# Attention feeding a gated MLP on one core: DMA transposes moved ahead of a store, score units moved by one place, batch 1 reordered, the last products in single banks

## Chip, cores, metric

One Trainium2 chip, one core. The metric is the device time of one execution in microseconds (us). Kernels that are compared ran on the same chip in alternating rounds. A ratio is the mean time of one kernel's runs over that of the other's runs of the same rounds, so it is not quite the ratio of the medians quoted beside it. The clock quoted with a run is the mean share of full speed that was granted to TensorE.

Engine names: PE is TensorE, PEld its weight loads, DVE VectorE, ACT ScalarE, POOL GpSimd, SP SyncE, which issues nearly all DMAs. SPq is the SP queue.

## The reference, cut

```python
# attention: q (8,16,384,64), k and v (8,4,384,64); 4 q heads share one kv head
attn = softmax(q @ k.T / sqrt(64));  a = attn @ v          # -> x (8, 384, 1024)
# gated MLP with a spatial mix over the sequence
h = relu(x @ w_in);  u, v = h[..., :512], h[..., 512:]
v_n = (v - mean(v)) / sqrt(var(v) + 1e-6)
v_s = einsum('ts,bsd->btd', w_spatial, v_n) + b_spatial
out = (u * v_s) @ w_out
```

## The kernel before

The eight batches overlap. While batch `b` computes its scores (18 "units": two matmuls on PE, then one exp on ACT), PE does the MLP of batches `c = b-1` and `d = b-2` between the units. Scores go through two PSUM buffers, so unit n needs the exp of unit n-2 to be over. Most products are made in two halves of 64 rows that run side by side; between the halves PE waits for a mark that POOL sets. q and k of batches 2 to 7 are cast by POOL and transposed by DMA, issued from SP.

```python
def batch(b, p, q, r, s):                 # p..s: PSUM banks
    group_uu(d, 2, 3, units(1, 3), (r, s))
    if more:
        cast_all_k(b + 1)
    unit(b, 3)
    value(c, 2, (p, q, r))
    # ... cut: units 4 to 12, value products, stores 1 and 2 of batch d,
    #          cast_all_q(b+1, 0), cast_all_q(b+1, 1), norm(c)
    if more:
        cast_v(b + 1, nc.gpsimd)
    group_voo(b, 0, d, 4, 5, units(13, 15), (p, s, r))   # its last copy issues store 3 of batch d
    if more:
        dma_transposes(b + 1)                            # k, q, q
    if b + 2 < B:
        load_all(b + 2)
    p, q, r, s = q, s, p, r
    group_sp(c, (units(15, 16), units(16, 17)), (p, q, r, s))

    def between():
        unit(b, 17)
        if more:
            unit(b + 1, 0)

    group_uu(c, 0, 1, between, (p, q))

# tail, last batch c: both spatial products of a pair share one two-bank tile
u_mm(c, 0)
sc = [ps_sc.tile([P, 2, 512], FP32, ...) for i in range(2)]
for m in range(NDT):
    sp_mm(c, m, sc[m // 2][:, m % 2, :])      # PE, 3 matmuls
    sp_add(c, m)                              # DVE
gate(c, 0)
for mu in range(1, NDT):
    u_mm(c, mu); gate(c, mu)
for i in range(6):
    o_mm(c, i)
    o_copy(c, i, nc.scalar if i % 2 else nc.vector, store_half=i >= 4)
```

The softmax here doesn't subtract the row's maximum and nothing guards it: scores larger than these inputs give would overflow.

## Time and profile before

| | before |
|---|---|
| median of four runs (range) | 278.56 us (277.77 to 279.52) |
| profiled span | 276.8 us |
| PE busy | 247.0 us, 89% |
| length of batches 2 to 6, from one batch's first value product to the next's | 30.05, 31.08, 31.41, 31.05, 32.34 us |

The lines that carry the argument stand in the prediction below. In a row of the table of waits the numbers are the sum in us, the times, and the longest. In a row of the timeline they are the start in us, the length in us, engine, line, operation, out<-in, and in brackets the idle time just before and what ended it. A row of the stretches gives from:to, the length, and the busy time of PE, PEld, DVE, ACT and POOL with counts, then the TensorE clock, the DMA share and GB/s.

### The profile page before, as it was taken

How to read it: one execution, taken by the hardware profiler on the slowest of the kernel's cores; microseconds unless marked ns; L12 is line 12 of the kernel's file. 1: busy time of each engine (PE TensorE's matmuls, PEld its weight loads, DVE VectorE, ACT ScalarE, POOL GpSimd, SP SyncE). 2: the span in 40 equal slices, each digit the busy share in tenths (PEclk: the TensorE clock that was granted, in tenths of full speed). 3: DMA queues.
4: the chain of work that ended last, by engine and by line, in shares of the span. 5: the costliest groups of instructions: out<-in, count | busy, mean ns of one | idle time of the engine just before them, and what ended most of it. 6: DMA issues, size and time to landing. Idle time of an engine off the chain costs nothing.

```text
span 276.8 us, 6011 instructions
## 1 busy us (share of the span) xinstructions
PE 247.0 (89%) x2529; PEld 116.2 (42%) x2529; DVE 150.0 (54%) x274; ACT 183.7 (66%) x228; POOL 47.9 (17%) x114
## 2 busy tenths in 40 slices
PE   2888698989997999899997999889995999989794
PEld 1232343544454444554454444554453444544351
DVE  2436569634584357625684357724683465836352
ACT  2978867879774787667774787668774777623402
POOL 3518114012300223012300123012300000000000
PEclk9999999999999999999999999999999999999999
DMA  8998999900129811693129811593229011100505
GB/s 220 279 315 209 238 254 234 321 14 11 69 117 255 267 78 76 169 291 104 78 116 233 290 78 75 164 297 103 79 108 188 0 78 75 79 2 0 229 0 227
DMA packets 57434, 41.66 MB, mean 151 GB/s; under 512 B 26816, under 2 KB 53568, under 8 KB 57408
## 3 DMA queue, kind: packets, MB, share of 16 engines
q1 hardware_dynamic: 53648, 37.89, 44.6%
q0 software_dynamic: 2720, 3.15, 6.9%
q8 instruction: 19, 0.31, 0.5%
q10 hardware_dynamic: 1040, 0.26, 0.4%
q14 instruction: 7, 0.06, 0.1%
HBM read 25.95 MB, written 12.58 MB: 139 GB/s over the span
## 4 chain that ended last, share of the span: by engine, by line
PE 78%; DMA 8%; DVE 6%; ACT 5%; issue 1%; SPq 0%; POOLq 0%; POOL 0%; ACTq 0%
PE sc L259 12%; PE po L491 11%; PE pv L451 11%; PE X L280 11%; PE pu L464 10%; DMA qT<-q 7%; PE sums L280 6%; PE psp L477 5%; ACT aT L270 4%; PE pv L319 4%; PE po L414 4%; PE pu L389 3%; DVE v_s L379 2%; DMA q<-in_q_dram 1%; DVE v_n L353 1%
## 5 line engine op out<-in xcount | busy, mean ns | idle before, releaser
L270 ACT ACTIVATE aT<-sc 128x1024 f16<-128x1024 f32 x144 | 141.2, 1023 | 53.6 <-PE sc L259 51.3
L259 PE MATMUL sc<-qT,kT 64*128 64x512 f16 x288 | 55.0, 392 | 14.9 <-DMA qT<-q 8.6
L491 PE MATMUL po<-w_out,gT 64*128 64x512 f16 x288 | 68.1, 376 | 0.0
L451 PE MATMUL pv<-w_in,xt 64*128 64x512 f16 x272 | 66.0, 376 | 0.0
L432 DVE COPY osb<-po 128x512 f32<-128x512 f32 x39 | 26.8, 688 | 30.3 <-PE po L491 26.7
L464 PE MATMUL pu<-xt,w_in 64*128 64x384 f16 x416 | 39.3, 323 | 2.0 <-DVE v_s L379 1.5
L401 DVE SCALAR_TENSOR_TENSOR gT<-pu,v_s 128x384 f16<-128x384 f32 x32 | 16.6, 553 | 41.3 <-PE pu L464 37.8
L307 DVE TENSOR_TENSOR xt<-X,rec 128x512 f16<-128x512 f32 x48 | 30.9, 686 | 12.5 <-ACT rec L299 11.0
L280 PE MATMUL X<-aT,v 128*32 128x512 f16 x576 | 36.5, 389 | 0.4 <-DVE osb L432 0.4
L259 PEld LDWEIGHTS <-kT 64*128 64x128 f16 x288 | 17.2, 94 | 43.7 <-issue 32.8
L528 POOL MEMSET mark<- 1x1 f32 x45 | 4.9, 108 | 165.4 <-PE po L491 87.6
L491 PEld LDWEIGHTS <-gT 64*128 64x128 f16 x288 | 25.5, 94 | 16.6 <-POOL mark L528 4.6
L451 PEld LDWEIGHTS <-xt 64*128 64x128 f16 x272 | 24.7, 94 | 14.1
L464 PEld LDWEIGHTS <-w_in 64*128 64x128 f16 x416 | 22.2, 94 | 17.2 <-issue 5.0
L168 POOL CAST q<-q 128x768 f16<-128x768 f32 (+2 forms) x32 | 23.6, 768 | 22.9 <-DMA q<-in_q_dram 21.4
L298 ACT ACTIVATE rec<-sums 128x512 f32<-128x512 f32 x24 | 14.5, 604 | 13.6 <-PE sums L280 13.6
L280 PEld LDWEIGHTS <-v 128*32 128x32 f16 x576 | 16.0, 99 | 16.9 <-issue 2.3
L280 PE MATMUL sums<-aT,ones 128*32 128x512 f16 x288 | 20.6, 392 | 0.1
L477 PE MATMUL psp<-wsT,v_n 64*128 64x384 f16 x168 | 18.7, 322 | 0.2 <-DVE wsT L206 0.2
L379 DVE TENSOR_TENSOR v_s<-psp,bias_b 128x384 f32<-128x384 f32 x28 | 16.9, 673 | 2.3 <-PE psp L477 2.3
L331 DVE TENSOR_SCALAR v_r<-pv 128x512 f32<-128x512 f32 x17 | 11.7, 691 | 9.5 <-PE pv L319 5.4
L340 DVE BATCH_NORM_STATS2 stats<-v_r 128x6 f32<-128x512 f32 x24 | 16.6, 690 | 0.2
(44 smaller groups left out, 165.7 us busy)
## 6 DMA issues: line engine op xcount, KB each, us to landing
out_dram<-osb SPq DMA_DIRECT2D x23, 512.0 KB, 2.7
q<-in_q_dram SPq DMA_DIRECT2D x14, 768.0 KB, 7.5
v<-in_v_dram SPq DMA_DIRECT2D x8, 384.0 KB, 8.6
k<-in_k_dram SPq DMA_DIRECT2D x7, 384.0 KB, 3.9
w_in<-in_moe_w_in_dram POOLq DMA_DIRECT2D x8, 256.0 KB, 7.6
q<-in_q_dram SPq DMA_DIRECT2D x2, 512.0 KB, 5.1
w_out<-in_moe_w_out_dram POOLq DMA_DIRECT2D x2, 512.0 KB, 14.4
ws<-in_moe_w_spatial_dram SPq DMA_DIRECT2D x1, 576.0 KB, 7.7
```

The costliest lines, as they stand in the source:

```text
L168: engine.tensor_copy(dst, src)
L259: mm = nc.tensor.matmul(sc[:, half, :], kT[b][lo:hi, gp, t, :], rhs[lo:hi, :], start=True, stop=True)
L270: nc.scalar.activation(aT[b, qt][:, gp, t], held["sc", b, u], AF.Exp, scale=scale)
L280: nc.tensor.matmul(dst[32 * g : 32 * (g + 1), :], weights(t, g), a[:, g // 2, t, g % 2, :], start=(t == 0), stop=(t == NST - 1),)
L307: nc.vector.tensor_tensor(xt[:, jj, :, qt * P : (qt + 1) * P], held["X", b, qt, jj].rearrange("p (j q) -> p j q", j=G), held["rec", b, qt] ...
L340: nc.vector.bn_stats(s6, held["v_r", b, st])
L379: nc.vector.tensor_tensor(held["v_s", b][:, m, :].rearrange("p (t s) -> p t s", t=NST), held["psp", b, m][:, 0:S].rearrange("p (t s) -> p ...
L432: nc.vector.tensor_copy(osb[:, cols], held["po", b, i])
L451: yield lambda kc=kc: nc.tensor.matmul(held["pv", b, st], xT[b][rows, kc, st * P : (st + 1) * P], w_in16[rows, kc, DH:DFF], start=(first a ...
L464: yield lambda kc=kc: nc.tensor.matmul(held["pu", b, mu][:, 0:S], w_in16[rows, kc, mu * P : (mu + 1) * P], xT[b][rows, kc, :], start=(firs ...
L477: yield lambda st=st: nc.tensor.matmul(held["psp", b, m][:, 0:S], held["v_n", b, st][rows, m * P : (m + 1) * P], wsT16[rows, st, :], start ...
L491: yield lambda m=m: nc.tensor.matmul(held["po", b, i], held["gT", b][rows, m, tt * P : (tt + 1) * P], w_out16[rows, m, half * 512 : (half ...
```

## The change

The intent: the transposes no longer stand behind a store that waits for compute; PE gets something to do in each short wait that is left. The core of the diff, cut:

```diff
 # part 1 and 2, batch()
-        group_uu(d, 2, 3, units(1, 3), (r, s))
+        group_uu(d, 2, 3, units(2, 4), (r, s))
         if more:
             cast_all_k(b + 1)
-        unit(b, 3)
         value(c, 2, (p, q, r))
 ...
             cast_v(b + 1, nc.gpsimd)
+            dma_transposes(b + 1)
         group_voo(b, 0, d, 4, 5, units(13, 15), (p, s, r))
-        if more:
-            dma_transposes(b + 1)
 ...
+        unit(b, 17)
+
         def between():
-            unit(b, 17)
             if more:
                 unit(b + 1, 0)
+                unit(b + 1, 1)
 # and the caller
-        banks = 0, 1, 2, 3
+        banks = 3, 0, 2, 1
 # part 3, batches 0 and 1: spatial weights cast by POOL, q/k transposes two to a bank,
 # a v product of batch 0 moved up, unit 16 ahead of a v product, unit (2, 1) added at the end
-            nc.vector.tensor_copy(
+            nc.gpsimd.tensor_copy(
                 ws16[:, tt, :, :], ws32[:, tt, :].rearrange("p (s t) -> p t s", t=NST)
 ...
-        for gp in range(NGP):
-            transpose_q(1, gp, 1)
+        transpose_q2(1, 1)
+        one[3]()
+        transpose_ws(0, 2)
         xmul(0, 2)
-        v_full(0, 1)
-        one[3]()
+        transpose_ws(2, 3)
 # part 4, tail
-        u_mm(c, 0)
-        sc = [ps_sc.tile([P, 2, 512], FP32, name=f"sc_sp_{i}", tag="sc") for i in range(2)]
+        sc = ps_sc.tile([P, 2, 512], FP32, name="sc_u", tag="sc")
+        u_mm(c, 0, sc[:, 0, :])
         for m in range(NDT):
-            sp_mm(c, m, sc[m // 2][:, m % 2, :])
+            sp_mm(c, m)
             sp_add(c, m)
-        gate(c, 0)
+            if m == 0:
+                gate(c, 0)
 ...
-        for i in range(2 * NST):
+        o_mm(c, 0, 0, 3)
+        o_mm(c, 1, 0, 3)
+        for i in range(2):
+            o_mm(c, i, 3, 4)
+            o_copy(c, i, nc.scalar if i % 2 else nc.vector)
+        for i in range(2, 5):
             o_mm(c, i)
-            o_copy(c, i, nc.scalar if i % 2 else nc.vector, store_half=i >= 4)
+            o_copy(c, i, nc.scalar if i % 2 else nc.vector, store_half=i == 4)
+        last_o(c, 5)      # two halves of 256 columns; the second stored from ACT's queue
```

More of the change, by code (lines that the diff above doesn't have):

```diff
@@ L199, in cast_ws, with transpose_ws @@
         loaded["ws16"] = ws16
-    def transpose_ws(st):
+    def transpose_ws(s0, s1):
         ws16 = loaded["ws16"]
-        psw = bank([P, NST, P], FP16, f"psw_{st}")
-        for tt in range(NST):
-            nc.tensor.transpose(psw[:, tt, :], ws16[:, tt, st, :], ident16)
-        nc.vector.tensor_copy(wsT16[:, st, :].rearrange("p (t q) -> p t q", t=NST), psw)
+        psw = bank([P, s1 - s0, NST, P], FP16, f"psw_{s0}")
+        for st in range(s0, s1):
+            for tt in range(NST):
+                nc.tensor.transpose(psw[:, st - s0, tt, :], ws16[:, tt, st, :], ident16)
+        nc.vector.tensor_copy(
+            wsT16[:, s0:s1, :], psw.rearrange("p s t q -> p s (t q)")
+        )
     def new_kT(b):
@@ L248, in transpose_q, with transpose_k2, transpose_q2 @@
         nc.vector.tensor_copy(qT[b, gp][:, qt], pq)
+    def transpose_k2(b):
+        k16 = loaded["k16", b]
+        pk = bank([P, NGP, NST, P], FP16, f"pk_{b}")
+        for gp in range(NGP):
+            for t in range(NST):
+                nc.tensor.transpose(
+                    pk[:, gp, t, :], k16[:, gp, t, :, :].rearrange("p h d -> p (h d)"), ident16
+                )
+        new_kT(b)
+        nc.vector.tensor_copy(kT[b], pk)
+    def transpose_q2(b, qt):
+        pq = bank([P, NGP, G, P], FP16, f"pq_{b}_{qt}")
+        for gp in range(NGP):
+            q16 = loaded["q16", b, gp]
+            for j in range(G):
+                nc.tensor.transpose(
+                    pq[:, gp, j, :], q16[:, qt, j, :, :].rearrange("p h d -> p (h d)"), ident16
+                )
+        for gp in range(NGP):
+            if (b, gp) not in qT:
+                new_qT(b, gp)
+            nc.vector.tensor_copy(qT[b, gp][:, qt], pq[:, gp])
     def score_mm(b, u):
@@ L384, in sp_add, with u_mm @@
         )
-    def u_mm(b, mu):
-        pu = bank([P, 512], FP32, f"pu_{b}_{mu}")
+    def u_mm(b, mu, dst=None):
+        pu = bank([P, 512], FP32, f"pu_{b}_{mu}") if dst is None else dst
         for kc in range(NKT):
@@ L408, in gate, with o_mm @@
         )
-    def o_mm(b, i):
+    def o_mm(b, i, m0=0, m1=NDT):
         tt, half = i // 2, i % 2
-        po = bank([P, 512], FP32, f"po_{b}_{tt}_{half}")
-        for m in range(NDT):
+        if m0 == 0:
+            held["po", b, i] = bank([P, 512], FP32, f"po_{b}_{tt}_{half}")
+        for m in range(m0, m1):
             nc.tensor.matmul(
-                po,
+                held["po", b, i],
                 held["gT", b][:, m, tt * P : (tt + 1) * P],
@@ L420, in o_mm @@
             )
-        held["po", b, i] = po
     def o_copy(b, i, engine=None, store_half=False):
@@ L437, in o_copy, with last_o @@
             nc.sync.dma_start(rows, osb)
+    def last_o(b, i):
+        tt, half = i // 2, i % 2
+        osb = held["osb", b, tt]
+        rows = out[b].rearrange("(p t) d -> p t d", t=NST)[:, tt, :]
+        for n in range(2):
+            cols = slice(half * 512 + n * 256, half * 512 + (n + 1) * 256)
+            po = bank([P, 256], FP32, f"po_{b}_{tt}_{half}_{n}")
+            for m in range(NDT):
+                nc.tensor.matmul(
+                    po,
+                    held["gT", b][:, m, tt * P : (tt + 1) * P],
+                    w_out16[:, m, cols],
+                    start=(m == 0),
+                    stop=(m == NDT - 1),
+                )
+            if n:
+                nc.scalar.activation(osb[:, cols], po, AF.Copy)
+                nc.scalar.dma_start(rows[:, cols], osb[:, cols])
+            else:
+                nc.vector.tensor_copy(osb[:, cols], po)
+                nc.sync.dma_start(rows[:, cols], osb[:, cols])
     LO, HI = slice(0, D), slice(D, P)
@@ L655, in first_batch @@
             if vi == 8:
-                for gp in range(NGP):
-                    transpose_k(1, gp)
-                    transpose_q(1, gp, 0)
+                transpose_k2(1)
+                transpose_q2(1, 0)
+                v_mm(0, 1)
+                relu(0, 1, nc.vector)
+                stats(0, 1)
+                cast_ws()
     def load_all(b):
@@ L690, in second_batch @@
         one[2]()
-        for gp in range(NGP):
-            transpose_q(1, gp, 1)
+        transpose_q2(1, 1)
+        one[3]()
+        transpose_ws(0, 2)
         xmul(0, 2)
-        v_full(0, 1)
-        one[3]()
+        transpose_ws(2, 3)
         load_all(2)
@@ L703, in second_batch @@
         one[5]()
-        for gp in range(NGP):
-            transpose_q(1, gp, 2)
-        cast_ws()
+        transpose_q2(1, 2)
         one[6]()
@@ L712, in second_batch @@
         norm(0)
-        for st in range(NST):
-            transpose_ws(st)
         one[8]()
@@ L719, in second_batch @@
         group_sp(0, one[11:13])
+        dma_transposes(2)
         value(1, 1)
@@ L722, in second_batch @@
         xmul(1, 1)
-        dma_transposes(2)
         load_all(3)
@@ L730, in second_batch @@
         group_uu(0, 0, 1, between)
+        one[16]()
         v_full(1, 1)
-        one[16]()
         one[17]()
         unit(2, 0)
+        unit(2, 1)
     def batch(b, p, q, r, s):
```

## The prediction

> **What bounds the kernel now.** I read the page first (busy shares, slices), then the table of who waited for whom, the timeline of one steady batch with the DMA issues in it, the busy times stretch by stretch, and last the timeline of the end.
>
> ```profile
> span 276.8 us, 6011 instructions
> PE 247.0 (89%) x2529; PEld 116.2 (42%) x2529; DVE 150.0 (54%) x274; ACT 183.7 (66%) x228; POOL 47.9 (17%) x114
> ...
> PE   2888698989997999899997999889995999989794
> ```
>
> PE is the one engine near full, and in the row of slices it is at 8 or 9 almost everywhere: PE sets the pace, ACT at 66% does not. So the kernel gains only where PE stands idle, 30 us in all (276.8 less 247.0). Six of those are the loads at the start, about three the last store; neither is touched except the last store a little. The rest, from the table of waits:
>
> ```profile
> PE sc L259 <- DMA qT<-q: 8.6, 5, 2.7
> PE sc L259 <- ACT aT L270: 4.7, 10, 0.9
> PE sc_sp L367 <- DVE v_s L379: 1.6, 2, 0.8
> PE pu L464 <- DVE v_s L379: 1.5, 6, 0.3
> PE pv L319 <- DVE xt L307: 1.2, 1, 1.2
> PEld L414 <- DVE gT L401: 0.5, 1, 0.5
> ```
>
> The first line is the large one: in five places (batches 2 to 6, each preparing the next) the first scores of a batch wait for the DMA transpose of q. The timeline of one of them shows why:
>
> ```profile
> 143.79 0.34 SPq L437 DMA_DIRECT2D out_dram<-osb  x1
> ...
> 144.23 1.40 SPq L218 DMA_TRANSPOSE kT<-k  x1
> ...
> 145.71 0.32 PE L464 MATMUL pu<-xt,w_in 64*128 64x384 f16 x1
> 146.17 2.99 SPq L225 DMA_TRANSPOSE qT<-q  x2
> 146.29 1.46 PE L464 MATMUL pu<-xt,w_in 64*128 64x384 f16 x15 [0.26 <-DVE v_s L379]
> 147.44 0.52 PE L259 MATMUL sc<-qT,kT 64*128 64x512 f16 x2
> ...
> 149.69 0.39 PE L259 MATMUL sc<-qT,kT 64*128 64x512 f16 x2 [1.73 <-DMA qT<-q]
> ```
>
> The SP queue issues in program order. The batch's last store stands ahead of the transposes and can't go before DVE has copied the last product at 143.76; only then come k (1.40 us of issue) and q (2.99 for two). The q data land 3.4 us after 146.17, PE having run dry at 147.96. What the transposes read was ready long before: POOL ended its casts of q at 136.07 (cast of 1.60 us at 134.47), and SP stood idle from 138.33, after the batch's second store (137.97, 0.36 us).
>
> ```profile
> 118.28:149.69 31.41, 29.31 (x328) 14.06 (x329) 17.46 (x31) 22.33 (x27) 5.69 (x14) 1.00 0.51 157
> ```
>
> This row (length of the stretch, then PE busy) says that a steady batch of 31.41 us has 29.31 us of PE and 2.1 us of idle, of which the wait above is 1.73 and the 0.26 is nearly all the rest. There is no second hole behind the first.
>
> **What the Trainium skill says.** "DMA: Bandwidth & Descriptors", section "Anatomy of one DMA — SWDGE (gpsimd) path", says that a semaphore wait happens on the issuing sequencer before dispatch, not in the DMA engines; the trace agrees: the 8.2 us from the last cast of q to the first transpose (136.07 to 144.23) went by behind a store that waited for DVE. The same page, "Rules for kernel authors", advises to issue a DMA early, compute, and wait on its semaphore late; here the issue-to-landing time is 3.3 to 4.8 us (median 3.5 for q), so an issue 7 us ahead hides it whole. "PSUM — Partial Sum Buffer", section "Terms", forbids two engines on the same bank and quadrant at once; different banks are not forbidden. In the tail the spatial product of the second block waits for DVE's read of the first though it writes the other bank of the two-bank tile: the waits of 1.6 us above are those of the tile's bookkeeping, not of a bank.
>
> **The change part by part.**
>
> (1) *Transposes ahead of the last store* (five times). The new SP order is store 2, k, q, q, store 3, loads; the engines' orders confirm that only this store moves. In the shown batch k can issue at 138.33, q at 138.33 + 1.4 + 0.1 = 139.8, landing by 139.8 + 3.5 = 143.3, the second q 1.5 later. Need: 147.4. Slack some 4 us, so even a landing of 4.8 us or the store's traffic beside it does not matter. The 8.6 us of waits go whole, as PE then has the second half of its products at hand. What the next loads do is better too: they start at 144.2 instead of 149.2, when the transposes are over.
>
> (2) *Score units shifted.* Unit 17 now stands ahead of the pair of u products, and units 0 and 1 of the next batch lie between its halves (before: 17 and 0), then 2 and 3 (before: 1, 2, and 3 by itself). The number of score matmuls is the same; unit 17's pair of 0.21 us fills the 0.26 us in which the second u product waits for DVE to free its bank. Six batches x 0.2 = 1.2 us. In the last batch nothing lies between the halves any more, so the wait for the mark (0.49 us after the last load in the trace) is bare there: minus 0.2. Net 1.0. ACT must keep up: exps of 16 and 17 would run 145.20 to 147.27, score 1 of the next batch needs 17's buffer at 147.65. It fits by 0.4 us.
>
> (3) *Batch 1* (about 28 to 62 us). A value product of batch 0 (8 matmuls, 1.90 us) moves up beside the transposes of batch 1, whose copies by DVE now run under it; this removes 0.88 us of idle before the first scores. The 1.22 us wait for the x multiply ahead of the same product goes, but the next product (of the third block) now waits for that multiply, sooner in time: I keep 0.5 of it. The casts of the spatial weights (three, 1.90 us) leave DVE for POOL, where at 0.5 to 0.7 us each they fall in a stretch in which it waits 4.14 us for k; so the multiply ahead of batch 1's own value product comes earlier, and the three weight copies (0.87 us) no longer hold the spatial product (0.23 and 0.51 us of waits). Following ACT, DVE and PE through the new order by hand I get the spatial product some 1.6 us sooner. Behind it, units 17, 0, 1 stand in a row where 16, 17, 0 did: the wait of 0.90 us for ACT stays. Net 1.5.
>
> (4) *Tail.* The four spatial products went in 259.63 to 263.49, 3.86 us, for 12 matmuls that take 0.163 us each back to back, or 1.95: with a bank each, 1.9 us are saved (the listed waits are 1.6; the rest is pipeline fill). DVE's chain after it (four additions of 0.66, one gate of 0.55 us) ends at about 263.5, and the first u product ends at 262.9, so gate 1 follows it closely, and the later gates follow PE again. The first two output products now run three steps each before they need the last gate: 6 x 0.213 = 1.28 us of work cover a wait of 0.6. The last product is cut into two halves of 256 columns: ACT copies 512 columns in 0.60 and 1024 in 1.02 us, so 256 in about 0.39 (an estimate from the two): 0.2 sooner, and its store of 128 KB from ACT's own queue may land 0.2 sooner than one of 256 KB (2.3 us). Sum 1.9 + 0.6 + 0.4 = 2.9.
>
> Sum: 8.6 + 1.0 + 1.5 + 2.9 = 14.0. No part adds work to PE (the same matmuls, but for 8 of 256 columns in place of 4 of 512 at the very end). 278.15 - 14.0 = 264.15; I say 264.2, since the profiled span and the timed runs differ by a constant of about 1.4 us that stays.
>
> **Rivals.** (a) *The wait moves to ACT.* With the hole gone, PE asks for score buffers sooner, and there are two. For it: 4.7 us of waits of scores for exps already exist, and the margin in (2) is 0.4 us. Against it: in a steady batch ACT is busy 22.33 us of what would be 29.4, and every listed wait of PE on ACT of any size lies in batches 0 and 1. If it comes, at most 0.5 us in each of five batches: 266.7. (b) *The transposes land no sooner*, because they meet the second store (512 KB, 2.7 us) on the same rings, or wait for something on POOL behind the casts (the v cast ends at 136.84, the mark comes at 140.84). The waits name PE and POOL, and the table can't tell which POOL instruction; were it the mark, k would issue at 141.0 and q land at 146.0, still ahead of 147.4. So this costs nothing or, with both delays, 1 us a batch: 269. (c) *The tail's new order loses itself to DVE*: the gate of the first block now stands between the additions and delays the last three by 0.55 us. PE waits for the banks of the first three, free by 262.9, and u 3 asks at 264.2. No loss. (d) *Batch 1 turns on ACT*: the first exps of batch 1 start about 0.8 us later (30.7 for 29.94), and if ACT bounds this stretch the gain of (3) goes: 265.7. ACT idles 8.8 us in 24 to 62 us, which speaks against.
>
> **Range and chances.** Part (1) is near certain and alone gives 3.1%, 269.5. (2) is likely, (3) the least certain (0 to 2.5), (4) worth 2 to 3.2. Low: all at their best and the transposes' later waits better by one more: 262.2. High: (3) nil, rival (a) in full: 267.5. Faster by over 2% means under 272.6: to miss it, over half of part (1) must fail. 0.95, with 0.04 for the same and 0.01 for slower.
>
> **What would show it.** In the profile after: no wait of scores for the q transposes, or under 1 us in all; k and q transposes issued right after the second store, the third store behind them; steady batches of 29.2 to 29.7 us with the same 29.3 us of PE busy; the wait of u products on the bias additions near zero; in the tail the spatial products in about 2 us without DVE waits. Wrong would be: batches still at 31 us (then a wait of the transposes that I have not seen), scores waiting for exps by over 2 us more than before, or a first score of batch 2 no earlier than before (then (3) gave nothing).

## The result and the profile after

The changed kernel took 264.9 us (median of four, 264.45 to 265.26) against 278.56; the ratio is 0.9507, 95% interval 0.9471 to 0.9544. Executions over 1.5% slower than the fastest of the same kernel are left out of the means.

From the page after: the span, the busy times, and PE's row of slices.

```profile
span 263.0 us, 6020 instructions
...
PE 244.5 (93%) x2533; PEld 115.3 (44%) x2533; DVE 146.5 (56%) x270; ACT 183.4 (70%) x228; POOL 49.6 (19%) x117
...
PE   2797989989999999999999999999999999999993
```

PE's busy time hardly moved (244.5 for 247.0 us), the span fell by 13.8: the gain is idle time. From the tenth slice on every one but the last is at 9. Of PE's table of waits the lines over half a microsecond in total, without those of the first loads:

```profile
PE sc L286 <- ACT aT L297: 4.3, 10, 0.9
...
PE pu L513 <- DVE v_s L406: 1.5, 6, 0.3
PE psw L206 <- DVE xt L334: 1.2, 1, 1.2
PE sc L286 <- DVE qT L251: 1.0, 2, 0.5
PE pv L346 <- DVE xt L334: 0.7, 2, 0.4
```

The 8.6 us of waits for the q transposes are gone, the line is not in the table, and no other has grown to take their place (the largest new one, the 1.2 us of `psw`, is in batch 1; see e9). The wait of u products for the bias additions (v_s) is unchanged at 1.5, though. The timeline of the batch that answers to the one shown of before:

```profile
133.55 0.36 SPq L464 DMA_DIRECT2D out_dram<-osb  x1
...
134.03 1.37 SPq L221 DMA_TRANSPOSE kT<-k  x1
...
135.52 3.37 SPq L228 DMA_TRANSPOSE qT<-q  x2
...
139.38 0.34 SPq L464 DMA_DIRECT2D out_dram<-osb  x1
...
141.02 0.44 PE L286 MATMUL sc<-qT,kT 64*128 64x512 f16 x2
...
141.30 0.32 PE L513 MATMUL pu<-xt,w_in 64*128 64x384 f16 x1
...
141.87 1.46 PE L513 MATMUL pu<-xt,w_in 64*128 64x384 f16 x15 [0.25 <-DVE v_s L406]
...
143.03 0.74 PE L286 MATMUL sc<-qT,kT 64*128 64x512 f16 x4
```

The transposes follow the second store at once, and the third store comes behind them at 139.38, as soon as its data are copied. The first score of the next batch comes at 143.03 in PE's own order, with nothing in brackets: q had been issued 7.5 us earlier. The same batch as a stretch:

```profile
118.81:148.12 29.31, 29.00 (x333) 13.82 (x336) 17.45 (x31) 22.34 (x28) 5.71 (x14) 1.00 0.61 183
```

29.31 us for 31.41, with 0.3 us of idle left. Where the 13.8 us of the span come from, by one and the same instruction in both traces (start of a value product, whose first matmuls are called sums):

| stretch | before | after | difference |
|---|---|---|---|
| start to value product 1 of batch 0 | 21.95 | 22.35 | +0.40 |
| from there to batch 2's first value product | 40.15 | 38.98 | -1.17 |
| from there over batches 2 to 6 | 155.93 | 145.42 | -10.51 |
| batch 7, to the tail's value product | 29.67 | 28.97 | -0.70 |
| from there to the end | 29.10 | 27.28 | -1.82 |

The first row is noise of the first loads: that point came between 20.87 and 22.35 us in the traces of all these kernels. So where tenths matter, the experiments below are read from such stretches, and the medians beside them.

### The profile page after: what moved, and what is told of

Read it like the earlier page. It is cut to its first block, busy times and chain, and to the rows that moved or that the text cites. A ratio compares the mean times of both kernels' runs of the same rounds, so it can differ in the third digit from the quotient of the medians.

```text
span 263.0 us, 6020 instructions
## 1 busy us (share of the span) xinstructions
PE 244.5 (93%) x2533; PEld 115.3 (44%) x2533; DVE 146.5 (56%) x270; ACT 183.4 (70%) x228; POOL 49.6 (19%) x117
## 4 chain that ended last, share of the span: by engine, by line
PE 85%; ACT 6%; DVE 5%; DMA 1%; issue 1%; POOLq 0%; ACTq 0%
PE pu L513 13%; PE sc L286 12%; PE po L540 12%; PE pv L500 12%; PE X L307 11%; PE sums L307 7%; PE pv L346 5%; ACT aT L297 5%; PE psp L526 4%; PE po L442 4%; DVE v_s L406 3%; PE pu L416 3%; DMA q<-in_q_dram 1%; PE psp L394 1%; DVE xt L334 1%
## 5 line engine op out<-in xcount | busy, mean ns | idle before, releaser
L286 PE MATMUL sc<-qT,kT 64*128 64x512 f16 x288 | 54.1, 392 | 5.8 <-ACT aT L297 4.3
L513 PEld LDWEIGHTS <-w_in 64*128 64x128 f16 x416 | 20.5, 94 | 18.7 <-POOL mark L577 4.3
L406 DVE TENSOR_TENSOR v_s<-psp,bias_b 128x384 f32<-128x384 f32 x32 | 19.5, 669 | 6.6 <-PE psp L394 3.4
```

Source lines behind the costliest of these rows:

```text
L286: mm = nc.tensor.matmul(sc[:, half, :], kT[b][lo:hi, gp, t, :], rhs[lo:hi, :], start=True, stop=True)
L406: nc.vector.tensor_tensor(held["v_s", b][:, m, :].rearrange("p (t s) -> p t s", t=NST), held["psp", b, m][:, 0:S].rearrange("p (t s) -> p ...
L513: yield lambda kc=kc: nc.tensor.matmul(held["pu", b, mu][:, 0:S], w_in16[rows, kc, mu * P : (mu + 1) * P], xT[b][rows, kc, :], start=(firs ...
```

## The experiments

All gave correct results. The experiments used three chips, one for each group of four in time (e1, e2, e3, e5; then e4, e6, e7, e9; then the last four); "before" is the kernel before on the same chip.

| label | what it is | median us | before us | ratio |
|---|---|---|---|---|
| e1_ahead | before + part 1 | 269.56 | 279.02 | 0.9664 |
| e2_shift | before + part 2 | 282.57 | 279.02 | 1.0134 |
| e3_both | before + parts 1 and 2 | 267.77 | 279.02 | 0.9616 |
| e5_actstore | before, third store from ACT's queue | 268.77 | 279.02 | 0.9648 |
| e4_behind | after without part 1 | 277.1 | 279.03 | 0.9942 |
| e6_tail | before + part 4 and a free bank | 276.62 | 279.03 | 0.9912 |
| e7_nosplit | after, last product whole | 264.44 | 279.03 | 0.9498 |
| e9_xmul | after, multiply first on DVE | 263.79 | 279.03 | 0.9463 |
| after_again | after | 264.71 | 279.07 | 0.9455 |
| e10_castv | e9 + cast of v later on POOL | 263.2 | 279.07 | 0.9415 |
| e11_all | e10 + last product whole | 263.11 | 279.07 | 0.9416 |
| e12_units | e11 + units at batch 2 as before | 262.66 | 279.07 | 0.9374 |

e2, e4 and e6: the 95% intervals of their ratios are 1.0108 to 1.0159, 0.9905 to 0.9979 and 0.9873 to 0.9951. What is said of them rests on their traces.

### e1_ahead: the transposes alone

```diff
             cast_v(b + 1, nc.gpsimd)
+            dma_transposes(b + 1)
         group_voo(b, 0, d, 4, 5, units(13, 15), (p, s, r))
-        if more:
-            dma_transposes(b + 1)
```

> The kernel before with part 1 alone: the k and q transposes issued ahead of the batch's third store, nothing else. Theory (the transposes stood behind a store that waited for DVE): no score waits for them any more, 8.6 us of waits go, and with each of the five stops a drain and refill of PE of some 0.17 us: 268.5 to 269.7 us, steady batches 29.5 to 29.8 us long. Rival (the wait turns into one for ACT or for landing transposes): over 271.5 us, with scores waiting for exps or for q by 3 us or more.

269.56 us, within the theory's range. PE waits for no q, and its list of waits has no line that before did not have. Batches 2 to 6 took 146.49 us for 155.93, so part 1 is worth 9.44 us: the 8.6 us of listed waits and about 0.17 for each of five stops, in which PE counts as busy, presumably while it drains and fills. A steady batch is 29.54 us, with 29.15 us of PE busy where before had 29.31:

```profile
90.42:119.96 29.54, 29.15 (x332) 13.81 (x336) 17.47 (x32) 22.23 (x28) 5.70 (x14) 1.00 0.58 154
```

### e5_actstore: another way to free the head of the queue

```diff
         elif half == 1:
-            nc.sync.dma_start(rows, osb)
+            (nc.scalar if tt == 2 and b < B - 2 else nc.sync).dma_start(rows, osb)
```

> The kernel before, its order of issue kept, but each batch's third store issued from ACT's queue, so that SP is not held by it. Theory (head of the SP queue is the whole cause): the transposes issue right after the second store, scores don't wait for q, the time falls as with part 1 alone, less a little for ACT, which now waits for DVE: 268.5 to 270.5 us. Rival (the transposes are slow or late for a reason of their own, such as POOL or the DMA engines): 275 or more.

268.77 us, the theory. The program order is that of before, but the third store leaves from another queue. The same batch in its timeline, first of SPq, then of ACT's queue:

```profile
133.72 0.36 SPq L437 DMA_DIRECT2D out_dram<-osb  x1
134.16 1.41 SPq L218 DMA_TRANSPOSE kT<-k  x1
135.67 2.92 SPq L225 DMA_TRANSPOSE qT<-q  x2
```

```profile
139.55 0.34 ACTq L437 DMA_DIRECT2D out_dram<-osb  x1
```

The transposes start 0.44 us after the second store, 5 us before the third. So it was the store at the head of the SP queue and not the DMA engines, POOL or the place in the program that held them.

### e2_shift: the score units alone

```diff
-        group_uu(d, 2, 3, units(1, 3), (r, s))
+        group_uu(d, 2, 3, units(2, 4), (r, s))
-        unit(b, 3)
 ...
+        unit(b, 17)
         def between():
-            unit(b, 17)
             if more:
                 unit(b + 1, 0)
+                unit(b + 1, 1)
 # and unit(2, 1) after unit(2, 0) at the end of batch 1
```

> The kernel before with part 2 alone: the score units one place along. Theory: the transposes land when they did, so PE only comes to the wait 0.2 us earlier and waits that much longer; waits for q grow to 9.2 to 10 us in all, the time falls by 0.3 to 0.8 us, from the last batch alone: 277.4 to 278.2. Rival (the shift is worth some 0.4 us in every batch by itself, as the batches of the changed kernel suggest): 275.5 to 276.

282.57 us: both expectations missed, the kernel got slower by 1.3%. The waits for q are 9.3 us in all, as the theory had it, and three of the batches are as long as expected (31.05 for 31.08, 30.94 for 31.05, 29.90 for 30.05). But two of them took 33.16 and 33.79. Their waits, in the timeline, and the 3.5 us that followed each, as stretches (the eighth number, behind POOL, is the clock); the third stretch follows a wait of 1.58 us:

```profile
150.37 0.69 PE L259 MATMUL sc<-qT,kT 64*128 64x512 f16 x4 [2.01 <-DMA qT<-q]
...
215.09 0.61 PE L259 MATMUL sc<-qT,kT 64*128 64x512 f16 x4 [2.64 <-DMA qT<-q]
```

```profile
150.37:153.87 3.50, 3.50 (x24) 2.09 (x26) 0.22 (x1) 1.94 (x2) 0.00 (x0) 0.56 0.98 260
215.09:218.60 3.51, 3.51 (x24) 1.98 (x26) 0.36 (x1) 1.94 (x2) 0.00 (x0) 0.58 0.22 50
118.90:122.40 3.50, 3.50 (x42) 2.19 (x44) 1.02 (x2) 2.00 (x3) 0.17 (x2) 1.00 0.93 258
```

After waits of 2.01 and 2.64 us the clock fell to about half, and PE did 24 matmuls where it otherwise does 42. Such an event costs some 1.7 us. Against before, these two batches are 1.75 and 1.45 us longer, the other three together 0.29 shorter, and batch 1 is 0.49 longer (40.64 us for 40.15, from value product 1 of batch 0 to batch 2's first), because unit (2, 1) stands third in a row there (see e3). That makes 3.4 us, as the medians have it (3.55). The shift alone sends unit 17 ahead, so PE comes to the wait earlier and waits longer: 2.01 us in place of 1.73 in that batch. All four of its runs had a clock of 0.987 or 0.988. The Trainium skill's page "TensorE: Matmul & The Clock Gate" (Part 1) describes such a gate: half rate after an idle window of about 3.4 us, and the windows run freely, that is, they don't start with the wait. The traces agree on the length of the window (see e4), but here 2.0 us of waiting in one were enough.

### e4_behind: the changed kernel without part 1

```diff
-            dma_transposes(b + 1)
         group_voo(b, 0, d, 4, 5, units(13, 15), (p, s, r))
+        if more:
+            dma_transposes(b + 1)
```

> The changed kernel with part 1 undone: the transposes again behind the third store. Theory: scores wait for q 9 to 10 us in five places again and each wait costs a refill beside: 274.5 to 276 us where the TensorE clock stays full; and since a wait of 2 us or more halved the clock for some 3.5 us in the run of the shift alone, each such event adds 1.7 us, up to three of them: 280 at most. Rival (the gain of the change is spread over its parts, and the order of SP is worth under 6 us once the others are in): below 271.

277.1 us, the theory with two clock events. Waits for q came to 9.5 us, two of them of 1.98 and 2.81 us, followed by mean clocks of 0.63 and 0.64 over 3.5 us; the run's clock was 0.987. So without part 1 hardly anything is left of the whole change (ratio 0.9942). This is not because the other parts are worth nothing: in this trace batch 1, batch 7 and the tail are 1.16, 0.70 and 1.82 us shorter than in before, as in the changed kernel, but batches 2 to 6 are 3.18 longer, about what two clock events cost.

Over the four traces with such waits (before, e2, e4, e6) six waits were of 1.98 us or more, and after five of them the clock fell; after the sixth, 2.65 us in the trace of before, it stayed at 1.00. After 1.58 and 1.80 us it stayed at 1.00 too, and the lengths of the other batches show no loss.

What decides it is in the clock records of the traces. They change only on a grid of 3.413 us. In all fourteen traces, from 20 us on, every step of this grid in which PE stood idle for 1.98 us or more, as the profile counts it, was followed by half rate, and none with 1.73 us or less was; in mid-kernel the half rate lasted one step, which costs 1.71 us. In e2 the steps from 147.36 and from 212.21 hold 2.01 and 2.64 us of idle, and the clock is 0.50 in the whole step after each. (The means of 0.56 to 0.64 above come from stretches that are not laid on the grid.) The wait of 2.65 us in before lies across a grid line at 211.39, with 1.28 us of idle in the step before the line and 1.69 in the one after. So where a wait falls on the grid decides, and the grid doesn't start with the kernel: its first line lies 0.0 to 3.2 us after the start of the span in these traces.

In the timed runs of the kernel before the clock lies between 0.987 and 1.0 and the time of its fast runs between 277.6 and 282.3 us (0.994 is about one event in 277 us, 0.987 two); on the third chip four of its ten fast runs lay at 281.6 to 282.3 us with 0.987 or 0.988. Part 1 takes these waits away, and the changed kernel's clock was 0.998 to 1.0 in all its ten runs. That fits its ratio, 0.9507 in the first rounds and 0.9455 beside the slower runs of before on the third chip; no run isolates the clock from the wait, and a clock of 0.994 to 0.997 also occurs in single runs of e7, e10 and e11, which have no wait for q.

### e3_both: parts 1 and 2

The edit is that of e1 and e2 together.

> The kernel before with parts 1 and 2. Theory: the two add up to what the traces of before and after show from batch 2 to the start of the tail, 11.2 us: 266.5 to 267.5 us, steady batches 29.3 us. Rival: the last 0.4 us per batch come from elsewhere (batch 1's new order and its banks): then no better than with part 1 alone by over 1 us.

267.77 us, a little over the range, steady batches 29.31 us as expected. Batches 2 to 6 gain 1.07 us over part 1 alone, 0.2 in each. Batch 1 gives most of it back: from value product 1 of batch 0 to batch 2's first it took 40.69 us for 39.94, because unit (2, 1) now stands third in a row there and waits for an exp. So part 2 is worth about 0.3 us, and this only once the transposes are early. Batch 7 stayed at 29.68 us: the 0.70 us that the changed kernel gains there are not from the shift.

### e6_tail: the tail alone, with a free bank

The tail of the changed kernel in the kernel before, and one line more:

```diff
         c, d = B - 1, B - 2
+        turn[0] = 0
         for mu in (2, 3):
             u_mm(d, mu)
```

> The kernel before with the changed tail alone, and with the first u product of the tail put in a bank that is free (the bank renumbering of the change does that; without it the product goes into the bank whose gate DVE has not read). Theory: the last steady batch to the tail's value product shortens by 0.7 us (the bank), and from there to the end by 1.8 (the spatial products in 1.95 us instead of 3.86; the split of the last store gives nothing): 275.5 to 276.3 us. Rival (the 0.7 us come from the score shift): then the bank changes nothing and the time is 276.3 to 277.

276.62 us, 0.3 over the theory's range, with a clock of 0.993 or 0.994 in three of four runs (the one at 0.997 took 275.12). The stretches are clear: from the last batch's second value product to the tail's 15.58 us for 16.29, so 0.71 from the bank; from there to the end 27.27 for 29.1, so 1.83 from the tail. The bank's line in the waits of before, which is in neither this kernel's nor the changed one's:

```profile
PE pu L389 <- DVE gT L401: 0.7, 1, 0.7
```

By the rotation `p, q, r, s = q, s, p, r` the banks 0, 1, 2, 3 end with p = 3 and q = 2 after six batches; the tail takes the bank after q, which is p, whose gate DVE has not read yet. From 3, 0, 2, 1 it ends with p = 1, and the tail gets a free one. The renumbering in the diff, which looks like bookkeeping, is a part of the change by itself, the fifth.

The tail's spatial products, before and then after:

```profile
259.63 0.65 PE L367 MATMUL sc_sp<-wsT,v_n 128*128 128x384 f16 x3
...
261.03 1.14 PE L367 MATMUL sc_sp<-wsT,v_n 128*128 128x384 f16 x6 [0.75 <-DVE v_s L379]
...
263.00 0.65 PE L367 MATMUL sc_sp<-wsT,v_n 128*128 128x384 f16 x3 [0.84 <-DVE v_s L379]
...
263.49 0.81 PE L389 MATMUL pu<-xt,w_in 128*128 128x384 f16 x4
```

```profile
247.65 2.11 PE L394 MATMUL psp<-wsT,v_n 128*128 128x384 f16 x12
...
249.60 0.65 PE L416 MATMUL pu<-xt,w_in 128*128 128x384 f16 x3
```

3.86 us became 1.95. That is all of part 4's gain, and more.

### e7_nosplit: the last product whole

```diff
-        for i in range(2, 5):
+        for i in range(2, 6):
             o_mm(c, i)
-            o_copy(c, i, nc.scalar if i % 2 else nc.vector, store_half=i == 4)
-        last_o(c, 5)
+            o_copy(c, i, nc.scalar if i % 2 else nc.vector, store_half=i >= 4)
```

> The changed kernel with its last output product whole again: one ACT copy of 512 columns and one store of 256 KB from SP. Theory (three stores at the end, one of them from a second queue, end later than two): from the start of the last copy to the end 3.8 us as before, against 4.06; in all 264.5 to 264.9 us, the same or 0.3 us faster than the changed kernel. Rival (the split saves the 0.2 us of the shorter copy and some of the store): 265.2 to 265.6.

264.44 us. From the start of the last copy to the end it took 3.8 us, against 4.1 in the changed kernel and 3.8 in the one before. The copy of the half is shorter (0.38 us for 0.60), but three stores instead of two land in the same microsecond, the halves after 2.5 and 2.6 us although they are half as large (2.3 us for 256 KB), and the end came 1.05 us after the last landing instead of about 0.9. So the split costs 0.3 us. The medians' difference from the changed kernel's on another chip is of the size of the noise; the verdict rests on the traces: from the tail's value product to the end the three kernels with the changed tail but no split (e7, e11, e12) took 27.08 us each, and the six with it 27.33 to 27.40. That it is the third store, and not the second queue, was not tried apart.

### e9_xmul and e10_castv: what batch 1 still waits for

In the table of waits after, 1.2 and 0.7 us are PE waiting for an x multiply (`xt`) in batch 1. They are two multiplies; the 0.7 us belong to batch 1's own and stayed in e9 to e12. The other one, of batch 0's last block, could start at 34.22 us, after ACT's reciprocal, but started at 35.51, behind three copies on DVE, two of q and one of spatial weights:

```profile
34.27 0.76 DVE L275 COPY qT<-pq 128x512 f16<-128x512 f16 x2 [1.83 <-PE pq L269]
...
35.03 0.56 DVE L207 COPY wsT<-psw 128x768 f16<-128x768 f16 x1
35.51 1.28 DVE L334 TENSOR_TENSOR xt<-X,rec 128x512 f16<-128x512 f32 x2
```

e9 puts it ahead of them:

```diff
+        xmul(0, 2)
         transpose_q2(1, 1)
         one[3]()
         transpose_ws(0, 2)
-        xmul(0, 2)
```

> The changed kernel with the x multiply of batch 0's last block put ahead of the copies of batch 1's q and of the spatial weights in DVE's order. Theory (this multiply, held up from 34.22 to 35.51 us by two copies, is what the next product waits for): it starts right after the reciprocal, the product some 1.2 us sooner, and 0.8 to 1.3 us of it are left at batch 2: 263.6 to 264.2 us. Rival (ACT's exps or the loads set this stretch): no change, 264.6 to 265.2.

263.79 us, but the theory's step failed in the trace: the next product began at 35.43 instead of 36.84, 1.25 us sooner without the 0.16 us by which this trace was ahead already (value product before it at 31.07 for 31.23), and at batch 2 nothing was left of it (value product at 61.40 for 61.33). The profiled run was the slowest of the six (265.3 us, the others 262.4 to 264.5); whether the faster ones lost it too, no trace shows. The timeline of e9 a little later shows the place where it went:

```profile
46.55 0.83 POOL L153 CAST v<-v 128x768 f16<-128x768 f32 x1 [5.89 <-DMA v<-in_v_dram]
...
47.32 0.23 POOL L577 MEMSET mark<- 1x1 f32 x2
...
47.47 0.66 PE L526 MATMUL psp<-wsT,v_n 64*128 64x384 f16 x6 [1.30 <-POOL mark L577]
```

POOL also did its work in program order here: its cast of v waited 5.89 us for a load, and the mark that PE needs stood behind the cast. It is the same fault as that of the store before the transposes, one engine further. e10 moves the cast behind the marks:

```diff
         cast_all_q(2, 1)
-        cast_v(2, nc.gpsimd)
 ...
         group_sp(0, one[11:13])
+        cast_v(2, nc.gpsimd)
```

> The multiply first, as before, and POOL's cast of batch 2's v moved behind the spatial group in POOL's order. Theory (the 1.4 us of the multiply were lost because POOL, waiting for the load of v, held the mark that PE waits for): no wait of the spatial products for the mark, batch 2's first value product 1.0 to 1.4 us sooner after the same start, 263.3 to 264 us. Rival (the loads bound this stretch anyway): the wait comes back as another one and the time stays within 0.3 us of the changed kernel.

263.2 us (changed kernel beside it: 264.71); the wait for the mark is gone, and the stretch from batch 0's value product to batch 2's took 37.72 us for 38.98. So the gain of the multiply, 1.26 us, is kept whole.

### after_again, e11_all, e12_units: a faster version

> The changed kernel once more, as the measure for the three beside it on the same chip: 264.4 to 265.3 us, TensorE clock 0.999 or 1.0 in nearly all runs.

264.71 us, clock 0.998 to 1.0, as expected.

e11 is e10 with e7's end.

> The same with the last output product whole: a further 0.3 us at the end: 263.0 to 263.7 us.

263.11 us, in range, and not to be told from e10 by the medians (263.2). From the tail's value product on it took 27.0 us for 27.3 in e10's trace.

e12 is e11 with, for batch 2 only, units 1 and 2 between the first halves and 3 after, and no unit (2, 1) at the end of batch 1:

```diff
-        unit(2, 1)
 ...
-        group_uu(d, 2, 3, units(2, 4), (r, s))
+        group_uu(d, 2, 3, units(1, 3) if b == 2 else units(2, 4), (r, s))
+        if b == 2:
+            unit(b, 3)
```

> The same, and only at the start of batch 2 the score units in the order of before (two units, not three, in a row ahead of its first u products). Theory: the wait of 0.90 us of the third unit for its buffer goes: 262.2 to 262.9 us. Rival (the wait moves behind the u products): no change.

262.66 us, in range; the stretch of batch 1 fell from 37.72 to 37.04 us, so 0.68 of the 0.90. A wait of 0.30 us of another unit for its exp remains there, and batch 2 itself kept its 28.17 us. This is the best version: ratio 0.9374, against 0.9455 for the changed kernel in the same rounds, 2 us.

## Why the prediction was right

The time, 264.9 for 264.2, the range and the direction are right. By its own steps, with the sizes that the traces gave:

- **Part 1, 8.6 us predicted, 9.4 measured.** The mechanism holds in full: e1 shows the gain, e5 shows that the head of the SP queue is the cause. What the step left out is the drain and refill at each stop, 0.17 us, which the profile counts as busy PE. It also left out the clock: in those executions of before where a wait halved it, more was to be gained, by 1.7 us each time.
- **Part 2, 1.0 predicted, about 0.3 measured.** The 0.2 us a batch came true (29.54 to 29.31). What failed is that the step counts no loss in batch 1: the shift puts a third unit in a row at the end of it and loses 0.75 us there. The wait of 0.90 us for ACT did stay, as part 3 says, but it is the shift that keeps it: e12, without it there, is 0.68 us faster. And the check "the wait of u products on the bias additions near zero" failed: it is 1.5 us before and after, as it ends with DVE's second addition in either case. The unit fills a gap before the first u matmul: three pairs of spatial products of 0.163 us from 144.94 end their issue at 145.43, the first u product came at 145.71, and the list shows no wait since the ends of the matmuls before lie over the gap.
- **Part 3, 1.5 predicted, 1.7 measured** (e3's stretch of 40.69 us against 38.98). The size agrees; the way did not quite. The spatial product came 1.35 us sooner after value product 1 of batch 0, not 1.6. The prediction kept 0.5 us of the 1.22 us of waiting for the multiply; all of it was still there, moved to the weight transposes (1.25 us). e9 and e10 show that the multiply was held by DVE's copies, and that moving it is worth another 1.3 us.
- **Part 4, 2.9 predicted, 1.8 measured.** The spatial products gave the 1.9 us to the tenth. "Cover a wait of 0.6" was mis-sized: the bracket of 0.5 was idle of the weight loads, while PE's matmuls lost only 0.17 us between the third (267.38 plus 3 x 0.216 = 268.03) and the next at 268.20. "0.2 sooner, and its store of 128 KB from ACT's own queue may land 0.2 sooner" was right about the copy (0.38 us for 0.60, though the 1.02 us of its estimate is that of an exp) and wrong in sum: the split cost 0.3 (e7).
- **What it missed:** the bank renumbering, 0.7 us (e6). It is in the diff and in the table of waits (the line of 0.7 us on `gT`), but the prediction didn't put the two together. It made good most of what part 4 lacked.
- **The rivals.** (a), ACT taking over the wait, did not happen in any steady batch: no wait of scores for exps from batch 2's second half on. (b), a late landing, neither. (c), a loss in the tail's DVE chain, did not come. (d), ACT bounding batch 1, did not take the gain; the order on DVE and POOL held it more (e9, e10). But PE still waits 2.0 us for exps there after the change, and e12's 0.68 us came out of such a wait.

The sum was right partly because errors cancelled: 0.8 too little in part 1 and 0.7 for the bank against 0.7 and 1.1 too much in parts 2 and 4, with 0.4 of start noise. That is luck in the sum, not in the mechanism of its largest term. The constant of 1.4 us between span and timed run was not one either: it compares two executions, and within the profiled run of the changed kernel it is 2.3 us (265.26 and 263.0). Still open is why the wait in batch 6 was always the longest (2.64 to 2.81 us in four traces).

## What to carry to other kernels

A queue or an engine that works in order hands on the wait of its head: look for what stands in front of an instruction in program order, not only for what it reads, and put the instruction whose operands come late behind those whose operands are ready. A stall costs more than its listed time, by drain and refill and, here from some 2 us within one step of the clock's grid, by the clock, so a small change that lengthens a stall can cost more than it saves. Undo or add one part at a time and read stretches between the same two instructions: with noise of a microsecond in the first loads, medians don't show parts of tenths.

## What the Trainium skill lacked or had wrong

- "TensorE: Matmul & The Clock Gate" (Part 1) gives an idle window of about 3.4 us, running freely, before the clock halves. The length is that of the traces (3.41 us), but the window need not be idle throughout: 1.98 us of idle in one were enough, 1.73 were not. A wait of 2.65 us that lay across two windows did not halve the clock.
- "DMA: Bandwidth & Descriptors" gives bandwidths for DMA transposes, but no time from issue to landing for one within SBUF of these sizes. Here k took 1.4 us of the SP queue and each q about 1.5, and q landed 3.3 to 4.8 us after its issue in the kernel before; beside the loads of batch 1 one q transpose of the changed kernel took 12.7 us to issue and 17.2 to land.
- The same page ("Issuing engines are not separate DMA queues") says that issuing from several engines saves only the time to initiate, usually small. e5 shows a larger use: a store that waits for compute, moved to another queue, freed the SP queue and saved 3.5% (ratio 0.9648).
